# Two product tiles of a sliding-window attention added by an accumulating DMA before TensorE sums them

## The chip, the cores and the metric

The kernel runs on one NeuronCore of a Trainium2 chip. A core has TensorE (PE, matrix products; its weight loads are listed as PEld), VectorE (DVE), ScalarE (ACT), GpSimd (POOL) and SyncE (SP), which run side by side and wait for one another by semaphores. The tensor memory that the engines work in (SBUF, 128 partitions) is filled and emptied by 16 DMA engines; matrix products land in eight banks of PSUM. The metric is the device time of one execution in microseconds; lower is better.

## The reference

One input `x` of 2048 tokens by 1024 features feeds two branches, mixed by a gate:

```python
g = sigmoid((x * gate_w).sum(-1, keepdims=True))
out = g * attention(x, wqkv, wo) + (1 - g) * ffn(B_x, w_gate, w_up, w_down)
# attention: 32 heads of 32; token s looks at s, s-2, ..., s-14 (8 places), where they exist
logits = einsum("bhsd,bhswd->bhsw", q, kg) * Dh ** -0.5     # kg: k gathered at those places
o = einsum("bhsw,bhswd->bhsd", softmax(masked logits), vg)  # then o @ wo
# ffn: (gelu(x @ w_gate) * (x @ w_up)) @ w_down, 3584 hidden features
```

All matrices are bf16. In the kernel both branches work on the same x.

## The kernel before

**Units.** The products of x with the weights are made in 78 units. Each unit makes two tiles of 128 features for 1024 tokens (a half, `s` = 0 or 1) by a scheme with seven products of 4 matmuls each instead of eight. Units 0 and 1 belong to the feed-forward branch; units 2 to 9 make q and k of the first 1024 tokens (one head tile `t` = 0 to 7 in each), units 10 to 17 those of the second half, units 18 to 25 make v, and the rest are feed-forward units. In unit b the order on TensorE is: first product (`p1`, L376, followed by ScalarE's copy L384), two products of the unit before (`p73`, L398, followed by VectorE's L403 that adds and evicts them), one product (`p5`), then a *slot* for one waiting job of another kind (L1260), small jobs for the gate (`gate_chunk` in units 8 and 10), two products (`p26`), and the last product of the unit before (`p4`, L406). q and k are kept in SBUF and stored by GpSimd's queue for a remainder (L529, L530).

**Logits.** For each head tile, VectorE multiplies q with the eight shifted copies of k: three blocks of 256 tokens per half (`ND` = 3), each a tile of 128 x 2048 (`qk_mult`, L598). The sum over the features of a head is made by TensorE against a pattern of ones (`reduce_mm`, L603): 4 matmuls for each block, which write 32 of the 128 output rows each and run beside one another, and which go on adding in the same PSUM bank over the eight head tiles. After two head tiles one slot job is queued; it sums the two tiles of the three blocks, 24 matmuls. A generator `qk_prods` waits until all pairs before it were summed. Six product tiles (`prod_tile`) go round. When all eight tiles of a half are summed, the softmax of that half begins. The fourth block of each half is done later (`spill`).

**Order of the work.** Every engine runs its instructions in the order in which the program emits them, and the program is written out by hand with a small planner: at the end of each unit `run_bg` gives background jobs (generators that emit VectorE work and report its estimated cost) a budget of 4.7 or 4.8 us, and 1.6 us more in a unit with a slot up to unit 21, 0.8 later, 0.6 for a gate job. Jobs go by priority (lowest number first), each from a unit on (`wake`), and some have a due unit at which what is left of them is emitted at once. The overdraft of a unit is taken from the next.

**Weight forms.** `t_forms` (lowest priority, 6) makes from the down and output weights in 9 steps the sums that a later product needs (L874), and GpSimd's queue stores them in DRAM (L877). `tf_load` fetches the weights for a step by SP's queue (L860), into one of three regions of 8 KB per partition that go round (`R_TF`, at 92, 100 and 108 KB) for the first five steps. At the end of unit 13 `tf_close` emits what is left of those five, and the v weights are loaded into the first two regions. VectorE later writes v's own sums from 108 KB on (`sums_v`, units 16 and 17).

**The end of the loop.** After unit 77 `run_last` and `down` multiply the feed-forward and attention results with the down and output weights; before that, VectorE folds the v products (L745, L752), multiplies the last feed-forward results (L254, L257) and scales blocks by the gate (L918).

Of the kernel before, what the change touches and what calls it, by code (L numbers as in the profile page):

```python
# [9 lines left out]
ALU = mybir.AluOpType  # L10
# [8 lines left out]
NWIN = 8  # L19
DIL = 2  # L20
HALO = 16
AC = 256
# [27 lines left out]
R_TF = (92, 100, 108)  # L50
R_TB = (16, 24)
# [2 lines left out]
R_VB = (40, 48.25)  # L54
R_AB = (44.25, 52.5)
R_PROD2 = 56.5
R_BUF = tuple(1 + 18 * k for k in range(10))
R_U2 = 181
R_QS = 189
# [9 lines left out]
def kernel(  # L69
# [12 lines left out]
    nc = tc.nc  # L82
# [7 lines left out]
    NT = KT  # L90
# [16 lines left out]
    def reg3(kb, a, b):  # L107
        return reg(kb, a * b).rearrange("p (a b) -> p a b", a=a)
# [9 lines left out]
    def bank(i):  # L118
        return banks[:, i, :]
# [17 lines left out]
    with tc.manual_schedule(engines={mybir.EngineType.PE, mybir.EngineType.DVE, mybir.EngineType.Activation,  # L137
# [55 lines left out]
        def flat(a):  # L193
            return a.rearrange("p a b -> p (a b)")
# [221 lines left out]
        now = [0]  # L416
# [17 lines left out]
        def bg(gen, prio, wake):  # L434
            t = Task(gen, prio, wake)
            tasks.append(t)
            tasks.sort(key=lambda t_: t_.prio)
            return t
# [41 lines left out]
        def at(n, fn):  # L480
            hooks.setdefault(n, []).append(fn)
# [10 lines left out]
        Q0 = 2  # L492
# [82 lines left out]
        kb = [reg3(R_Q + 9 * i + 4, NT, KV) for i in range(2)]  # L575
        vb = [reg3(R_VB[i], NT, KV) for i in range(2)]
        pr_off = [R_PR + 4 * i for i in range(4)] + [R_PROD + 4 * i for i in range(2)]
        prod = [reg3(o, NWIN, AC) for o in pr_off]
        attn_all = reg3(R_ATTN, NBLK, SC)
        mask = reg3(R_MASK, NWIN, SJ)  # L580
# [11 lines left out]
        def prod_tile():  # L592
            k = pr_n[0] % 6
            pr_n[0] += 1
            return prod[k]
# [5 lines left out]
        def reduce_mm(lg, src, start, stop):  # L601
            for j in range(NJ):
                nc.tensor.matmul(lg[32 * j:32 * j + 32, :], lhsT=R_[:], rhs=src[:, :, j * SJ:(j + 1) * SJ],  # L603
                                 start=start, stop=stop)

        ND = BPS - 1
        LGB = 5
        reduced, front, prods = [0], set(), {}

        def qk_prods(u, s, t):  # L610
            while reduced[0] < NT * s + t - t % 2:
                yield None
            out_ = []
            for a in range(ND):
                pr = prod_tile()
                qk_mult(pr, u.T[:, 0, a * AC:(a + 1) * AC], u.T[:, 1, a * AC:(a + 1) * AC])
                out_.append(pr)
                yield 1.14
            prods[t] = out_
            if t % 2:  # L620
                slotq.append(lambda: (qk_reduce(s, t - 1, prods[t - 1]), qk_reduce(s, t, out_)))

        def qk_reduce(s, t, out_):
            assert s == 0 or t > 0 or front == {0, 2}
            for a, pr in enumerate(out_):
                reduce_mm(bank(LGB + a), pr, t == 0, t == NT - 1)
            reduced[0] += 1
            if t == NT - 1:
                if s == 0:
                    bg(softmax(0, 2, LGB, 0), 1, now[0])  # L630
                    bg(softmax(2, 1, LGB + 2, 1), 1, now[0])
                else:
                    bg(softmax(BPS, 3, LGB, 2), 1, now[0])
# [3 lines left out]
            nc.sync.dma_start(out=kb[s], in_=k_d[s][:])  # L637

        def spill(s):
            while reduced[0] < 2 * NT:  # L640
                yield None
            accs = []
            temps = [prod_tile() for _ in range(2)]

            def mult(t, dst):
                qk_mult(dst, qb[s][:, t, :], kb[s][:, t, HALO:HALO + AC])

            def add(g, t):
                TT(out=accs[g], in0=accs[g], in1=temps[t % 2], op=ALU.add)

            for g in range(NT // QG):
                accs.append(prod_tile())
                mult(QG * g, accs[g])
                yield 1.14
                for t in range(1, QG):
                    mult(QG * g + t, temps[t % 2])
                    yield 1.14
                    if t > 1:
                        add(g, t - 1)
                        yield 1.14  # L660
                add(g, QG - 1)
                yield 1.2
            slotq.append(lambda: spill_reduce(s, accs))

        slotq = []
# [139 lines left out]
        QE = Q0 + 2 * NT  # L805
# [41 lines left out]
        NQ = NK // NP  # L847
        N1 = 5
# [1 line left out]
        TC = NQKV + 1  # L850

        def tf_set(q):
            o = R_TF[q % 3] if q < N1 or q >= N1 + 2 else R_TB[q - N1]
            return [reg3(o + NP * k, NP, SC) for k in range(4)]

        def tf_load(q):
            i0 = NP * q
            for k, a in enumerate(((0, 0), (0, 1), (1, 0), (1, 1))):
                for sl, src in r_parts(*a, i0, i0 + NP):
                    nc.sync.dma_start(out=tf_set(q)[k][:, sl.start - i0:sl.stop - i0, :], in_=src)  # L860
# [3 lines left out]
        def t_forms():  # L864
            for q in range(NQ):
                tf_q[0] = q
                if q in (N1 + 1, N1 + 2):
                    tft.prio = 3.9 if q == N1 + 1 else 4.5
                    tasks.sort(key=lambda t_: t_.prio)
                while q >= N1 and now[0] < (TB if q < N1 + 2 else TC) + 1:  # L870
                    yield None
                r11, r12, r21, r22 = tf_set(q)
                for o_, a, b_ in ((r11, r12, r11), (r12, r22, r12), (r22, r22, r11), (r21, r21, r22)):
                    TT(out=flat(o_), in0=flat(a), in1=flat(b_), op=ALU.subtract)  # L874
                    yield 0.71
                for k, t in enumerate((r11, r22, r12, r21)):
                    nc.gpsimd.dma_start(out=t_d[k][:, NP * q:NP * q + NP, :], in_=t)  # L877
                if q + 3 < (N1 if q < N1 else NQ if q >= N1 + 2 else 0):
                    tf_load(q + 3)

        at(Q0 + 1, lambda: [tf_load(q) for q in range(3)])
        at(TB, lambda: [tf_load(q) for q in range(N1, N1 + 2)])
        at(TC, lambda: [tf_load(q) for q in range(N1 + 2, min(N1 + 5, NQ))])
        tft = bg(t_forms(), 6, Q0 + 2)
# [65 lines left out]

        KX = int(R_P5A[0] - R_BUF[6])

# [296 lines left out]
        for b in range(n):  # L1249
            now[0] = b  # L1250
            for fn in hooks.pop(b, []):
                fn()
            cur = units[b]
            prv = units[b - 1] if b > 0 else None
            cur.p1()
            if prv:
                prv.p73()
            cur.p5()
            extra = 0.0
            if slotq:  # L1260
                slotq.pop(0)()
                extra += 1.6 if b <= QE + 3 else 0.8
            for fn in pre.pop(b, []):
                fn()
                extra += 0.6
            cur.p26()
            while actq and cur.kind != "up":
                actq.pop(0)()
            if prv:
                prv.p4()  # L1270
            for fn in post.pop(b, []):
                fn()
            run_bg(b, (4.7 if b < NQKV else 4.8) + extra)
            if b == n - 1:
                pre_down_4(0)
# [32 lines left out]
```

## Time and profile before

| | |
|---|---|
| median of 3 runs | 720.22 us (719.84 to 720.38) |
| profiled execution | 720.06 us, span 718.3 us |
| TensorE / VectorE / ScalarE / GpSimd busy | 707.2 / 673.2 / 328.7 / 134.5 us |
| granted TensorE clock | 1.00 |
| sum matmuls (L603) | 208, 13.1 us |
| product tiles of the logits (L598) | 64 of 1219 ns |
| SP's queue (q1) / GpSimd's queue (q0) | 105.46 MB / 48.29 MB |

The span is what the profile covers from the first to the last instruction; the execution's own time is 1.8 us longer. In a group's row the numbers after the bar are the busy time of the group (us), the mean of one instruction (ns), and the idle time of the engine before them with what ended it. In the timeline a row is: start (us), length (us), engine, line, operation, output and inputs, count, and in brackets the idle time before it and who ended it. A row of a stretch has its bounds, its length, the busy time of TensorE, its weight loads, VectorE, ScalarE and GpSimd with their counts, the granted clock, the share of the DMA engines' time and the GB/s. In the list of waits a row has the total, the number of times and the longest.

### The profile page before, as it was taken

The numbers are of one execution on the slowest core, as the hardware profiler recorded it, in microseconds if no ns is written. First come the engines' busy times: TensorE is split into PE (matmuls) and PEld (weight loads), VectorE is DVE, ScalarE is ACT, GpSimd is POOL, SyncE is SP. The second block draws the span as 40 slices with busy tenths as digits, with TensorE's granted clock in tenths as the row PEclk, the third lists the DMA queues.
The fourth block names the chain that finished last, engine by engine and source line by source line (L and its number), as shares of the span: only waits on it lengthen the run. The fifth ranks groups of instructions, "written<-read, shape, count | busy, mean of one in ns | idle before, by whom it ended". The sixth has DMA issues, their size and how long they took to land. (4 is left out here: it accounts for less than half of the span.)

```text
span 718.3 us, 10752 instructions
## 1 busy us (share of the span) xinstructions
PE 707.2 (98%) x4051; PEld 408.2 (57%) x4107; DVE 673.2 (94%) x722; ACT 328.7 (46%) x600; POOL 134.5 (19%) x233
## 2 busy tenths in 40 slices
PE   8999999999999999999999999999999999999998
PEld 4466656655544444444444444444447886758887
DVE  2789989999999999999999999999999999899997
ACT  4554546444456665555555555555322321131431
POOL 1323544133210332121300000000210002110011
PEclk9999999999999999999999999999999999999999
DMA  9976643378264758574934836371891899995951
GB/s 276 284 183 219 229 142 122 106 247 304 102 205 127 231 197 252 175 221 149 294 115 152 280 123 214 124 288 59 300 427 52 307 401 396 420 429 223 379 213 60
DMA packets 92276, 162.04 MB, mean 226 GB/s; under 512 B 19280, under 2 KB 68848, under 8 KB 87872
## 3 DMA queue, kind: packets, MB, share of 16 engines
q1 hardware_dynamic: 75520, 105.46, 42.7%
q0 software_dynamic: 15984, 48.29, 19.3%
q10 hardware_dynamic: 720, 7.60, 2.7%
q8 instruction: 32, 0.52, 0.3%
q14 instruction: 20, 0.16, 0.1%
HBM read 112.17 MB, written 54.14 MB: 232 GB/s over the span
## 5 line engine op out<-in xcount | busy, mean ns | idle before, releaser
L366 PE MATMUL banks<-arena 128*128 128x512 bf16 x2136 | 472.1, 379 | 4.2 <-DVE arena L403 0.7
L366 PEld LDWEIGHTS <-arena 128*128 128x128 bf16 x2184 | 240.5, 111 | 235.3 <-issue 7.0
L1046 PE MATMUL banks<-arena 128*128 128x256 bf16 x1260 | 138.9, 273 | 0.8 <-DVE arena L1012 0.6
L1046 PEld LDWEIGHTS <-arena 128*128 128x128 bf16 x1260 | 123.1, 98 | 16.7 <-issue 1.5
L389 ACT COPY arena<-banks 128x512 f32<-128x512 f32 x78 | 45.8, 587 | 130.7 <-PE banks L366 130.7
L403 DVE TENSOR_TENSOR arena<-banks,arena 128x1024 bf16<-128x1024 f32 x78 | 95.2, 1221 | 11.0 <-PE banks L366 5.5
L374 ACT CAST arena<-banks 128x512 bf16<-128x512 f32 x102 | 59.7, 586 | 42.4 <-PE banks L366 42.4
L745 DVE TENSOR_TENSOR arena<-arena 128x2048 bf16<-128x2048 bf16 x64 | 77.0, 1220 | 0.5
L752 DVE TENSOR_TENSOR arena<-arena 128x2048 bf16<-128x2048 bf16 (+2 forms) x96 | 73.9, 776 | 1.0
L598 DVE TENSOR_TENSOR arena<-arena 128x2048 bf16<-128x2048 bf16 x64 | 74.7, 1219 | 0.1
L260 POOL DMA_DIRECT2D h_d<-arena x28 | 20.4, 730 | 226.5 <-DVE arena L254 195.4
L1079 PE MATMUL banks<-arena 128*128 128x512 bf16 x282 | 62.5, 379 | 0.3
L396 ACT COPY banks<-banks 128x512 f32<-128x512 f32 x78 | 44.5, 570 | 21.8 <-PE banks L366 20.0
L1004 DVE TENSOR_TENSOR arena<-arena 128x2304 bf16<-128x2304 bf16 x40 | 53.3, 1352 | 0.5
L384 ACT COPY banks<-banks 128x512 f32<-128x512 f32 x78 | 45.0, 576 | 13.6 <-PE banks L366 12.1
L1051 ACT COPY banks<-banks 128x256 f32<-128x256 f32 x60 | 21.4, 356 | 60.9 <-PE banks L1046 60.7
L1079 PEld LDWEIGHTS <-arena 128*128 128x128 bf16 x288 | 28.2, 98 | 33.5
L927 DVE TENSOR_TENSOR arena<-arena 128x2048 bf16<-128x2048 bf16 (+1 forms) x40 | 41.8, 1111 | 1.3 <-DMA arena<-h_d 1.3
L372 ACT ACTIVATE arena<-banks 128x512 bf16<-128x512 f32 x54 | 32.2, 597 | 15.4 <-PE banks L366 15.3
L323 DVE TENSOR_TENSOR arena<-arena 128x1024 bf16<-128x1024 bf16 x60 | 38.6, 685 | 0.5
L1012 DVE TENSOR_TENSOR arena<-arena 128x2304 bf16<-128x2304 bf16 x28 | 37.7, 1351 | 0.2
L254 DVE TENSOR_TENSOR arena<-arena 128x2048 bf16<-128x2048 bf16 x28 | 34.0, 1216 | 1.9 <-ACT arena L251 1.4
(93 smaller groups left out, 435.8 us busy)
## 6 DMA issues: line engine op xcount, KB each, us to landing
arena<-t_d SPq DMA_DIRECT2D x8, 2304.0 KB, 14.4
h_d<-arena POOLq DMA_DIRECT2D x28, 512.0 KB, 4.3
arena<-w_c SPq DMA_DIRECT2D x12, 1152.0 KB, 14.1
t_d<-arena POOLq DMA_DIRECT2D x36, 256.0 KB, 4.3
arena<-h_d SPq DMA_DIRECT2D x6, 1536.0 KB, 12.7
arena<-in_B_w_gate_dram SPq DMA_DIRECT2D x15, 512.0 KB, 5.7
arena<-in_B_w_up_dram SPq DMA_DIRECT2D x15, 512.0 KB, 5.3
arena<-in_B_w_down_dram SPq DMA_DIRECT2D x28, 256.0 KB, 6.6
```

The source lines that it names most:

```text
L366: self.pe = nc.tensor.matmul(ps, lhsT=self.L[form](kt), rhs=rhs[:, kt, :], start=(start and kt == 0), stop=(kt == HK - 1), skip_group_chec ...
L374: nc.scalar.copy(out=o_, in_=i_)
L384: nc.scalar.copy(out=self.Y, in_=self.X)
L389: nc.scalar.copy(out=self.p5s, in_=self.V)
L396: nc.scalar.copy(out=self.Z, in_=self.Y)
L403: TT(out=self.T[:, :, c2s], in0=pair, in1=self.p5s.rearrange("p (o n) -> p o n", o=1).to_broadcast([P, 2, SC]), op=ALU.add)
L598: TT(out=dst, in0=q.rearrange("p (o s) -> p o s", o=1).to_broadcast([P, NWIN, AC]), in1=_win_ap(k, [[-DIL, NWIN], [1, AC]]), op=ALU.mult)
L745: TT(out=prod2[(t // 2) % 2][:, t % 2], in0=ab, in1=_win_ap(v[:, t, HALO:HALO + AC], [[SJ, NJ], [-DIL, NWIN], [1, SJ]]), op=ALU.mult)
L752: TT(out=out_, in0=h(0), in1=h(1), op=ALU.add)
L1004: TT(out=o_, in0=a, in1=b_, op=op)
L1046: nc.tensor.matmul(c(i, h, j), lhsT=l[:, kt, j * P:(j + 1) * P], rhs=r[:, kt, :], start=False, stop=(kt == KH - 1), skip_group_check=True)
L1079: nc.tensor.matmul(ps, lhsT=L[:, i, j * P:(j + 1) * P], rhs=R[:, i, :], start=(start and q == 0), stop=(q == NK - 1), skip_group_check=not ...
```

## The change

For the four pairs of head tiles of the first 1024 tokens, VectorE writes the products of the odd tile into three tiles of their own (`pr_tmp`, at 108 to 120 KB), and after each of them GpSimd's queue issues a DMA that adds this tile (512 KB, bf16) to the product tile of the even head tile. A job of cost 0 that wakes one unit later puts the pair's sum into the slot queue, so that the sum is emitted one unit later than before; it now has 12 matmuls instead of 24. The pairs of the second half are summed by 24 matmuls as before; the odd tile of its first pair is written to `pr_tmp` too. `qk_prods` may now run ahead of the sums by one pair in the first half and at the start of the second. The third region of the weight forms is given up for `pr_tmp`: the first five steps go round in two regions, two steps are loaded ahead and each further one after the step two before it. A slot of the first half grants 0.8 us to the planner instead of 1.6.

```diff
+R_TMP = 108
...
+        pr_tmp = [reg3(R_TMP + 4 * i, NWIN, AC) for i in range(3)]
...
         def qk_prods(u, s, t):
-            while reduced[0] < NT * s + t - t % 2:
+            pair, add = s * NT // 2 + t // 2, paired(s * NT // 2 + t // 2)
+            while len(reduced) < pair - int(pair <= NT // 2 or t % 2 == 0 and pair == NT // 2 + 1):
                 yield None
             out_ = []
             for a in range(ND):
-                pr = prod_tile()
+                pr = pr_tmp[a] if pair <= NT // 2 and t % 2 else prod_tile()
                 qk_mult(pr, u.T[:, 0, a * AC:(a + 1) * AC], u.T[:, 1, a * AC:(a + 1) * AC])
                 out_.append(pr)
+                if add and t % 2:
+                    nc.gpsimd.dma_start(out=flat(prods[t - 1][a]), in_=flat(pr), accum_op=ALU.add)
                 yield 1.14
             prods[t] = out_
             if t % 2:
-                slotq.append(lambda: (qk_reduce(s, t - 1, prods[t - 1]), qk_reduce(s, t, out_)))
...
+                if add:
+                    bg(later(lambda p=prods[t - 1]: qk_reduce(s, pair, [p])), -1, now[0] + 1)
+                else:
+                    slotq.append(lambda p=prods[t - 1]: qk_reduce(s, pair, [p, out_]))
+
+        def paired(pair):
+            return pair < NT // 2
+
+        def later(fn):
+            slotq.append(fn)
+            yield 0.0
+
+        def qk_reduce(s, pair, sets):
+            assert pair == len(reduced)
+            p = pair % (NT // 2)
+            assert s == 0 or p > 0 or front == {0, 2}
+            for k, out_ in enumerate(sets):
+                for a, pr in enumerate(out_):
+                    reduce_mm(bank(LGB + a), pr, p == k == 0, p == NT // 2 - 1 and k == len(sets) - 1)
+            reduced.append(pair)
...
         def tf_set(q):
-            o = R_TF[q % 3] if q < N1 or q >= N1 + 2 else R_TB[q - N1]
+            o = R_TF[q % 2] if q < N1 else R_TF[q % 3] if q >= N1 + 2 else R_TB[q - N1]
...
-                if q + 3 < (N1 if q < N1 else NQ if q >= N1 + 2 else 0):
-                    tf_load(q + 3)
...
+                m_ = 2 if q < N1 else 3
+                if q + m_ < (N1 if q < N1 else NQ if q >= N1 + 2 else 0):
+                    tf_load(q + m_)
...
-        at(Q0 + 1, lambda: [tf_load(q) for q in range(3)])
+        at(Q0 + 1, lambda: [tf_load(q) for q in range(2)])
...
-                extra += 1.6 if b <= QE + 3 else 0.8
+                extra += 1.6 if b <= QE + 3 and len(reduced) > NT // 2 else 0.8
```

More of the change, by code (lines that the diff above doesn't have):

```diff
@@ L607 @@
         LGB = 5
-        reduced, front, prods = [0], set(), {}
+        reduced, front, prods = [], set(), {}
         def qk_prods(u, s, t):
-            while reduced[0] < NT * s + t - t % 2:
+            pair, add = s * NT // 2 + t // 2, paired(s * NT // 2 + t // 2)
+            while len(reduced) < pair - int(pair <= NT // 2 or t % 2 == 0 and pair == NT // 2 + 1):
                 yield None
@@ L620, in qk_prods @@
             if t % 2:
-                slotq.append(lambda: (qk_reduce(s, t - 1, prods[t - 1]), qk_reduce(s, t, out_)))
[L623 to L628, printed above, removed]
+                if add:
[15 more added lines that the diff above has]
+            reduced.append(pair)
+            if p == NT // 2 - 1:
                 if s == 0:
@@ L639, in spill @@
         def spill(s):
-            while reduced[0] < 2 * NT:
+            while len(reduced) < NT:
                 yield None
```

## The prediction

> **What bounds the kernel now.** I read the page's busy times first, then who waited for whom on TensorE, the groups by line, and the timeline and the stretches of the part that is changed (48 to 118 us).
>
> ```profile
> PE 707.2 (98%) x4051; PEld 408.2 (57%) x4107; DVE 673.2 (94%) x722; ACT 328.7 (46%) x600; POOL 134.5 (19%) x233
> ...
> L598 DVE TENSOR_TENSOR arena<-arena 128x2048 bf16<-128x2048 bf16 x64 | 74.7, 1219 | 0.1
> ...
> L603 PE MATMUL banks<-arena,ones_r 128*32 128x512 bf16 x208 | 13.1, 381 | 0.0
> ```
> TensorE works 98% of the span and VectorE 94%: two engines are nearly full, and a gain on one lasts only while the other follows. All 208 sum matmuls cost 13.1 us, four at a time; the 48 that go are part of that.
>
> ```profile
> PE banks L366 <- DVE arena L403: 0.7, 2, 0.5
> ```
> That is the longest wait of the unit loop's matmuls: TensorE bounds it, VectorE is close behind.
>
> ```profile
> 57.36 3.49 DVE L598 TENSOR_TENSOR arena<-arena 128x2048 bf16<-128x2048 bf16 x3
> 57.74 0.56 POOL L529 DMA_DIRECT2D q_d<-arena  x1 [2.22 <-DVE arena L403]
> 58.29 0.56 POOL L530 DMA_DIRECT2D k_d<-arena  x1
> ...
> 60.52 0.57 ACT L384 COPY banks<-banks 128x512 f32<-128x512 f32 x1
> ...
> 62.26 1.23 DVE L403 TENSOR_TENSOR arena<-banks,arena 128x1024 bf16<-128x1024 f32 x1
> 62.95 0.98 PEld L603 LDWEIGHTS <-ones_r 128*32 128x32 bf16 x24 [0.38 <-issue]
> 62.95 1.48 PE L603 MATMUL banks<-arena,ones_r 128*32 128x512 bf16 x24
> ...
> 64.36 0.44 PE L366 MATMUL banks<-arena 128*128 128x512 bf16 x1
> ```
> This is the first pair's slot, in unit 6. The odd tile's three products end at 58.58, 59.72 and 60.85, and TensorE sums at 62.95. A slot of 24 matmuls takes 62.95 to 64.36, 1.41 us. It begins 2.43 us after the L384 copy that follows a unit's first product, and L384 recurs every 6.05 us (54.48, 60.52) without a slot.
>
> ```profile
> 55.00:60.00 5.00, 4.95 (x24) 3.31 (x24) 4.63 (x13) 2.19 (x5) 1.63 (x3) 1.00 1.08 355
> 60.00:65.00 5.00, 5.00 (x41) 2.76 (x40) 4.88 (x6) 1.56 (x5) 1.22 (x3) 1.00 0.08 28
> 76.60:90.70 14.10, 13.84 (x91) 8.73 (x95) 13.18 (x15) 6.82 (x15) 6.27 (x12) 1.00 0.57 185
> 520.00:600.00 80.00, 79.89 (x619) 60.58 (x619) 78.34 (x78) 21.91 (x52) 4.57 (x9) 1.00 0.76 303
> ```
> The last two columns are the DMA engines' share and GB/s. The queues are free right after 60, but over half full at 77 to 91, where later additions run. The last row gives the rate of full engines: 303/0.76 = 399 GB/s.
>
> **The change part by part.** *Removed:* 12 of 24 sum matmuls in four slots. At 1.41 us for 24, half is 0.70: 4 x 0.70 = 2.8 us off TensorE, which waits there for nothing (2.6 if some 0.05 a slot is fixed). VectorE's products stay the same 48 + 16.
>
> *Added: twelve additions of 512 KB on GpSimd's queue.* Issue: 0.54 to 0.86 us each on an engine that is 19% busy, hidden; behind them in GpSimd's order stand the q and k stores and the t stores. No addition by DMA is in the trace. Copying 512 KB takes all DMA engines 1.31 us at 399 GB/s; the h store that ran alone (487 to 491 us) held them 37.8% of 4 us, 1.51 us. An addition must fetch both tiles, so twice that: 2.6 or 3.0. From below, a plain copy: 1.3. From above, the transposing DMA that also handles its data: 13 of 128 KB (512 tokens by 128 features) in 18.48 us of SP's queue, 5.7 us per 512 KB. I take 2.6, since the destination is SBUF as for the loads of that row; 3.0, 1.3 and 5.7 stay for the range. The fixed part is 1.9 us: a q store of 64 KB lands 2.1 us (median) after its issue and moves for 0.2.
>
> The Trainium skill ("Collectives: The Full Stack", The bandwidth ceiling) says that a reduction runs at half the copy's rate because the add needs two source reads, not because adding costs cycles. By that the two-fold price holds; by the bare copy each addition would be 1.3 us and the sum 0.4 us lower. No run here has shown either.
>
> *Moved: each pair's sum goes one unit later* (units 7, 9, 11, 13), and this is the time that the DMA has. With half slots of 0.70 and the gate matmuls of units 8 and 10 at 0.71 (slot and gate together held 76.60 to 78.72), L384 of unit 7 falls at 66.72 (68.13 less 1.41), of units 9, 11, 13 at 80.23, 93.74, 106.54. The third tile's sum begins 2.43 + 0.47 later: 69.6, 83.1, 96.6, 109.4. The odd tile's first product ends at 58.6, and for the others 4.12 after L384 of units 7, 9, 11 (1.74 to L403, 1.14, 1.22): 70.8, 84.3, 97.9. Time allowed: 11.0, 12.3, 12.3, 11.6 us. Needed: 0.3 behind the k store + 1.9 + 3 x 2.6 = 10.0, plus what competes: nothing for the first (share 0.08); for the others the four 256 KB weight loads that the change puts there, 2.6 us at 399 GB/s, of which about 2.3, 2.3 and 2.0 fall beside them. Margins 1.0, 0.0, 0.0, -0.4: TensorE waits 0.4 us. Every 0.1 us on an addition adds 0.3 us to three or four pairs.
>
> *Weight forms with two buffers instead of three.* Sets 2, 3, 4 are loaded one form later, each behind t stores that stand in the software queue after the additions. At unit 9 the first form of set 3 comes at about 88 us, and its second load lands about then. VectorE may be 1.4 us late in a unit (L403 can start 1.74 after L384 and takes 1.22; TensorE needs it 20 matmuls, 4.4 us, after L384) and 2.1 with a gate. I take 0, bounds 0 and 2. The v weights wait for the t stores of set 4 at unit 13 as before (second load at 121.75, first use at 133.72): 6 us of cover.
>
> *Planner.* Four slots grant 0.8 us less background work, so 3.2 us of VectorE pieces slide back to the end of the loop, where VectorE has no room:
>
> ```profile
> 508.89 1.22 DVE L403 TENSOR_TENSOR arena<-banks,arena 128x1024 bf16<-128x1024 f32 x1
> ...
> 510.16 2.75 PE L366 MATMUL banks<-arena 128*128 128x512 bf16 x12 [0.28 <-DVE arena L403]
> ```
> Working the planner's accounts through, unit 76 gets one more v product and two more folds (1.1 + 0.7 + 0.4) ahead of this L403 and loses one scaling (1.1): L403 comes 1.1 us later against TensorE, and the 0.28 wait grows by up to that. I take 0.8, ends 0 and 1.1. Until there VectorE follows: from 145 to 505 us it stands idle before L403 and the softmax for some 6 us, more than 2.8. After the loop VectorE waits for the last h load until 534.10, while TensorE has work that needs none of it until 544.68. In the second half pair 5 sums in unit 16 instead of 17, with its products two units old; 0.
>
> *Sum:* -2.8 + 0.4 + 0.8 = -1.6 us. The profiled execution took 720.06 (span 718.3 and 1.8 around it), 0.16 under the median of 720.22: 718.5 profiled, **718.6** against the median.
>
> **Rivals.** (1) *The additions land late*: this one ends on the other side. Place: the half slots, where TensorE would wait for a DMA. At 3.0 us an addition the waits are 0.2 + 1.2 + 1.2 + 1.6 = 4.2; they also give VectorE its time, so without the 0.8: -2.8 + 4.2 = +1.4, 721.6. At 4.4 they are 21: 738. At 5.7, 36.6: 754. It takes the whole gain from about 2.8 us, and shows as slower from 3.0. For it: margins of nothing in three pairs, and the h store's 1.51. Against it: full-rate rows at 399 GB/s and a quiet queue after 60. (2) *VectorE gives the gain back*: it is at 235.6 of 240 us in the middle of the kernel, and with every earlier TensorE time met by a late L403, the saving shrinks to 0 to 1: 719.4 to 720.2. Against it: its idle before L403 is there to be eaten. (3) *The form loads stall VectorE* at units 9 and 13 by 5 us: beyond the cover of 2.1, 3 us each: -1.6 + 6 = 724.6. For it: the t stores now stand behind the additions. Against it: form work stands last in VectorE's order.
>
> **How the numbers follow.** A change under 0.2% (1.4 us) can't be told from none. In time, with its own range of 717.4 to 720: 0.43. A little late (2.8 to 4.4 us an addition): 0.26. Far late: 0.18. VectorE gives it back: 0.07. Form loads: 0.06. Predicted is the first case, the likeliest single one. About four in five of it end below 718.8: faster 0.35; its rest, rival 2 and a trace of rival 1 are the same: 0.16; slower 0.49. Range 717.4 (a plain copy's price, no loss at the end) to 738, which leaves out the far late additions.
>
> **What would show it.** Half slots of L603, 12 matmuls in 0.70 us, with no TensorE wait on a DMA before them; additions landing within 10 to 12.3 us of the first product's end, three in a row some 2.6 us apart; L403 near the end of the unit loop with a wait of about 1 us. Wrong if the additions land more than 3 us apart (rival 1), if L366 waits for L403 all along (rival 2), or if L874 waits for weight loads (rival 3).

## The result and the profile after

| | before | after |
|---|---|---|
| median | 720.16 us (4 runs, 719.84 to 720.38) | 729.04 us (4 runs, 727.60 to 729.83) |
| profiled execution | 720.06 us, span 718.3 | 729.21 us, span 727.1 |
| TensorE / VectorE / GpSimd busy | 707.2 / 673.2 / 134.5 us | 711.6 / 673.2 / 145.0 us |

The changed kernel takes 1.0121 times as long, with a 95% interval of 1.0104 to 1.0139: 8.9 us slower. A gain of 1.6 us was forecast. VectorE does the same work. TensorE's busy time grows although 48 matmuls are gone. A part of the growth is a stretch at half the clock (below). Another part is no work at all: 48 records of L366 are missing in the profile of before (2136 against 2184), and their time is not counted as busy. From 240 to 480 us, where TensorE's work is unchanged, the profile of before has 1097 matmuls and 238.84 us, that of after 1119 and 240.00. For the same reason the count of instructions does not show the 48.

The busy times of the page and the group of the product tiles, after:

```profile
PE 711.6 (98%) x4059; PEld 408.4 (56%) x4059; DVE 673.2 (93%) x722; ACT 328.9 (45%) x600; POOL 145.0 (20%) x245
...
L600 DVE TENSOR_TENSOR arena<-arena 128x2048 bf16<-128x2048 bf16 x64 | 74.8, 1219 | 0.1
```

The product tiles still take 1219 ns, so neither the added DMAs nor their issue slow these products. What is new stands in the list of TensorE's waits (total, times, longest; L605 are the sum matmuls, L367 the products of a unit, L283 the gate's matmuls, L1065 the matmuls behind the loop):

```profile
PE banks L605 <- DMA arena<-arena: 4.5, 3, 2.1
PE banks L1065 <- DVE arena L1031: 1.8, 2, 1.2
PE banks L367 <- DVE arena L404: 1.8, 2, 1.0
PE banks L283 <- ACT arena L390: 1.3, 2, 0.7
```

The first row is the additions: the sums of three tiles stand still for them. Before, L366's wait for L403 was 0.7 in all, and there was no wait of the gate's matmuls.

The stretches of the changed part, after (bounds, length, busy times of TensorE, weight loads, VectorE, ScalarE, GpSimd, then the granted clock, the DMA engines' share and GB/s):

```profile
76.60:90.70 14.10, 12.68 (x72) 7.51 (x71) 9.66 (x10) 6.75 (x15) 7.14 (x13) 1.00 0.99 269
60.00:80.00 20.00, 19.33 (x103) 12.07 (x102) 19.28 (x21) 9.66 (x22) 10.06 (x16) 1.00 0.95 215
80.00:100.00 20.00, 18.58 (x99) 11.27 (x97) 15.29 (x17) 9.04 (x21) 11.75 (x21) 1.00 1.01 256
100.00:140.00 40.00, 35.47 (x189) 21.16 (x188) 34.05 (x37) 17.70 (x34) 19.01 (x33) 0.96 0.77 232
```

From 60 to 100 us the DMA engines have hardly anything free: 0.95 and 1.01, where the kernel before shows 0.61 and 0.39; from 100 to 140 it is 0.77, before 0.36. The 76.60 row had 0.57 before. The GB/s rise less than the share, since an addition holds the engines for longer than the bytes counted for it.

The first pair's half slot, in the timeline after:

```profile
67.84 0.57 ACT L385 COPY banks<-banks 128x512 f32<-128x512 f32 x1
...
70.27 0.88 PE L605 MATMUL banks<-arena,ones_r 128*32 128x512 bf16 x12
```

It begins 2.43 us after L385, as forecast, and waits for nothing. The third tile of pair 2 (the pairs are counted from 0) waits, and so does the last pair, pair 3, here with the rows behind it:

```profile
102.91 0.40 PE L605 MATMUL banks<-arena,ones_r 128*32 128x512 bf16 x4 [2.07 <-DMA arena<-arena]
...
115.47 0.40 PE L605 MATMUL banks<-arena,ones_r 128*32 128x512 bf16 x4
116.26 0.40 PE L605 MATMUL banks<-arena,ones_r 128*32 128x512 bf16 x4 [0.38 <-DMA arena<-arena]
118.74 0.62 PE L605 MATMUL banks<-arena,ones_r 128*32 128x512 bf16 x4 [2.08 <-DMA arena<-arena]
...
119.29 3.02 PE L367 MATMUL banks<-arena 128*128 128x512 bf16 x8
```

In pair 3 the second and third tile wait 0.38 and 2.08 us. Then eight matmuls take 3.02 us (0.38 each), while elsewhere twelve take 2.75 (0.23 each). The granted clock says why, in the stretch of just this time (the last but two column):

```profile
118.10:121.50 3.40, 2.76 (x10) 1.05 (x10) 3.23 (x7) 0.25 (x1) 2.57 (x6) 0.50 0.97 354
```

It is at half from 118.1 to 121.5 us, for 3.41 us in the records.

**Where the 8.9 us are.** L384 (now L385) recurs once in a unit, so its distance from unit to unit, after less before, gives an account:

| place | us |
|---|---|
| start, up to unit 0 | +1.3 |
| four slots of 24 gone (1.56 each), four of 12 come (0.97 each) | -2.4 |
| gate matmuls in units of their own | +2.0 |
| unit 9: L404 late (wait 0.74) | +0.8 |
| sums wait for additions: 2.07 in unit 11, 0.38 and 2.08 in unit 13 (4.5, 4.8 with what restarts) | +4.8 |
| half clock in units 13 to 15 | +1.4 |
| waits of before that are gone (118.78 and 175.74 us, and a 0.1) | -0.9 |
| end of the loop (0.73) and behind it (1.15), less 0.1 | +1.8 |

A unit without a slot takes 6.05 us, with a slot of 24 it takes 7.61, with one of 12 it takes 7.02. The start is not the change: over the profiled executions of the kernels of this study the copy of unit 0 lies anywhere between 25.9 and 27.5 us, with 26.14 before and 27.41 after. It goes with the time at which the full clock is first granted: 8.9 to 9.3 us in the three executions with 27.4 or 27.5 (the change, runs 1 and 2 below), 4.0 to 7.2 in all others.

Three of these lines need the profile. First the gate in unit 8 and the form loads in unit 9, from the timeline after:

```profile
78.03 0.61 PE L283 MATMUL banks<-arena 128*32 128x512 bf16 x8 [0.67 <-ACT arena L390]
...
85.06 0.69 DVE L892 TENSOR_TENSOR arena<-arena 128x1024 bf16<-128x1024 bf16 x1 [3.84 <-DMA arena<-in_B_w_down_dram]
...
86.95 1.22 DVE L404 TENSOR_TENSOR arena<-banks,arena 128x1024 bf16<-128x1024 f32 x1
88.22 4.48 PE L367 MATMUL banks<-arena 128*128 128x512 bf16 x20 [0.74 <-DVE arena L404]
```

The gate's eight matmuls wait 0.67 us for ScalarE's copy of a bank (L390). Before, the slot's sum matmuls ran ahead of them and covered this wait. VectorE stands 3.84 us for a weight load of `tf_load`, then 0.60 for another; L404 is late, and TensorE waits. These loads were issued from 73.4 us on, beside the second pair's additions, and three of the four took 9.7 to 10.5 us. One issued at 103.58, when the additions had landed, took 3.0.

Second, GpSimd's own waits between 60 and 125 us, from the list of waits and the timeline after:

```profile
POOL z_d L288 <- DMA arena<-arena: 6.5, 3, 3.2
...
POOL t_d L895 <- DMA arena<-arena: 1.9, 1, 1.9
...
POOL k_d L531 <- DMA arena<-arena: 0.8, 1, 0.8
```

```profile
100.68 0.48 POOL L288 DMA_DIRECT2D z_d<-arena  x1 [3.23 <-DMA arena<-arena]
...
103.14 0.48 POOL L288 DMA_DIRECT2D z_d<-arena  x1 [1.98 <-DMA arena<-arena]
...
107.56 2.70 POOL L622 DMA_DIRECT2D arena<-arena  x3
```

The z stores read a small tile that no addition touches. The additions of pair 2 landed at 96.66, 100.40 and 102.86, and the z stores that leave 0.3 us after each stand eight places behind it in the queue. The trace's records show why. The DMAs of GpSimd's queue tell of their landing by eight semaphores that go round (numbers 111 to 118), and each DMA first waits for the one that had its semaphore before: the store at 96.94 waits for semaphore 115, which the addition issued at 89.85 raises. So it is the program that lets no ninth transfer of this queue start while the oldest of eight is under way. Before, the same eight go round. The queue stood 9.2 us behind additions in all; 6.5 of them, at the z stores, lie ahead of the last pair's additions, which left at 107.56, though the first odd product was ready at 101.78. Before, GpSimd's only wait for a transfer here is 0.6 us, of a load for the store whose data it reads.

Third, the end of the loop and the work behind it, after:

```profile
518.01 2.75 PE L367 MATMUL banks<-arena 128*128 128x512 bf16 x12 [1.01 <-DVE arena L404]
...
589.38 2.79 PE L1065 MATMUL banks<-arena 128*128 128x256 bf16 x24 [1.15 <-DVE arena L1031]
```

The first was 0.28 before; the second is new.

### The profile page after: what moved, and what is told of

Same layout as the page of the kernel before. It is cut to its first block, busy times and chain, and to the rows that moved or that the text cites. A ratio compares the mean times of both kernels' runs of the same rounds, so it can differ in the third digit from the quotient of the medians.

```text
span 727.1 us, 10734 instructions
## 1 busy us (share of the span) xinstructions
PE 711.6 (98%) x4059; PEld 408.4 (56%) x4059; DVE 673.2 (93%) x722; ACT 328.9 (45%) x600; POOL 145.0 (20%) x245
## 5 line engine op out<-in xcount | busy, mean ns | idle before, releaser
L367 PE MATMUL banks<-arena 128*128 128x512 bf16 x2184 | 476.2, 380 | 2.2 <-DVE arena L404 1.8
L367 PEld LDWEIGHTS <-arena 128*128 128x128 bf16 x2184 | 240.5, 111 | 236.9 <-issue 9.2
L1065 PE MATMUL banks<-arena 128*128 128x256 bf16 x1260 | 138.9, 273 | 1.8 <-DVE arena L1031 1.8
L1065 PEld LDWEIGHTS <-arena 128*128 128x128 bf16 x1260 | 123.0, 98 | 17.8 <-DVE arena L1031 1.4
L404 DVE TENSOR_TENSOR arena<-banks,arena 128x1024 bf16<-128x1024 f32 x78 | 95.2, 1221 | 15.1 <-PE banks L367 11.6
L390 ACT COPY arena<-banks 128x512 f32<-128x512 f32 x78 | 45.8, 587 | 130.8 <-PE banks L367 130.8
L600 DVE TENSOR_TENSOR arena<-arena 128x2048 bf16<-128x2048 bf16 x64 | 74.8, 1219 | 0.1
L385 ACT COPY banks<-banks 128x512 f32<-128x512 f32 x78 | 45.0, 576 | 13.6 <-PE banks L367 12.4
L1031 DVE TENSOR_TENSOR arena<-arena 128x2304 bf16<-128x2304 bf16 x28 | 37.8, 1355 | 0.2
```

Of the source, the lines that this page charges most:

```text
L367: self.pe = nc.tensor.matmul(ps, lhsT=self.L[form](kt), rhs=rhs[:, kt, :], start=(start and kt == 0), stop=(kt == HK - 1), skip_group_chec ...
L385: nc.scalar.copy(out=self.Y, in_=self.X)
L390: nc.scalar.copy(out=self.p5s, in_=self.V)
L404: TT(out=self.T[:, :, c2s], in0=pair, in1=self.p5s.rearrange("p (o n) -> p o n", o=1).to_broadcast([P, 2, SC]), op=ALU.add)
L600: TT(out=dst, in0=q.rearrange("p (o s) -> p o s", o=1).to_broadcast([P, NWIN, AC]), in1=_win_ap(k, [[-DIL, NWIN], [1, AC]]), op=ALU.mult)
L1065: nc.tensor.matmul(c(i, h, j), lhsT=l[:, kt, j * P:(j + 1) * P], rhs=r[:, kt, :], start=False, stop=(kt == KH - 1), skip_group_check=True)
```

## The experiments

Theories, by the names that the expectations use. *Crowding* or *engine* theory: additions and their neighbours share DMA engines that are full. *Issue* or *queue* theory: GpSimd's queue, behind the additions, sends stores and later additions too late. *Rhythm* theory: the loss comes from moving and halving the sums (gate matmuls, weight forms, half slots), with no part of the DMA. *Planner* theory: the end of the loop loses because a half slot grants 0.8 us instead of 1.6. The kernel before was timed with each group: 720.04, 720.06, 719.93 and 719.94 us. Waits, clocks and rows are those of the one profiled execution of a run; its time is given where it lies 1 us or more from the median.

**1. A plain copy instead of the addition.** The even tiles' products are lost; the DMA has one tile to read instead of two.

```diff
-  nc.gpsimd.dma_start(out=flat(prods[t - 1][a]), in_=flat(pr), accum_op=ALU.add)
+  nc.gpsimd.dma_start(out=flat(prods[t - 1][a]), in_=flat(pr))
```

> The changed kernel with the adding taken out of the twelve DMAs: each copies the odd tile over the even one (the even tiles' products are lost from the logits). Same issues, same bytes written, half the bytes read. Crowding theory (the additions hold the DMA engines 2.56 us each; weight loads and GpSimd's queue stand behind them): the copies land about 1.4 us apart, no TensorE wait on a DMA, the form wait of 4.4 us shrinks under 2, and of the 8.9 us over the kernel before 5 to 7 go: about 722 to 724. Rhythm theory (moved sums, gate matmuls without cover, planner order): hardly a change, 727 to 729. Issue theory (the twelve issues on GpSimd are the cost, whatever they move): 727 to 729 as well, with the same gaps in GpSimd's queue.

Measured: 721.64 us (10 runs; profiled 725.03, with a wait of 2.01 us at 367.74, far behind the changed part), 1.0028 [1.0016, 1.0041]. The copies of pair 0 land 1.48 and 1.47 us apart, those of pair 3 1.29 and 1.21, about half of what the additions of these pairs show. TensorE waits for none of the copies, the clock stays at 1.00, and the stretches from 60 to 100 us show how far the engines are from full:

```profile
60.00:80.00 20.00, 19.22 (x102) 11.99 (x103) 19.33 (x20) 9.61 (x22) 8.04 (x16) 1.00 0.78 281
80.00:100.00 20.00, 19.22 (x109) 11.54 (x109) 16.15 (x18) 9.67 (x22) 12.74 (x25) 1.00 0.80 276
```

Same queue, same moved sums, and twelve issues as before, though each takes GpSimd 0.54 us here and 0.89 with the addition: some 7 us of the 8.9 hang on what an addition costs beyond a copy, and that is above all the time that it holds the DMA engines.

**2. No DMA at all.** The odd tiles are computed and left out of the sums.

```diff
-  if add and t % 2:
-      nc.gpsimd.dma_start(out=flat(prods[t - 1][a]), in_=flat(pr), accum_op=ALU.add)
```

> The changed kernel without the twelve DMAs; the sums take the even tiles alone (the odd tiles' products of the first 1024 tokens are left out of the logits). What the halved and moved sums, the two form regions and the planner give by themselves. Crowding theory: -2.4 for the half slots, +1.5 for gate matmuls that now wait for a copy in units 8 and 10, +1 to 2 at the end of the loop: 720.5 to 722. Prediction's sum without any DMA: -2.8 + 0.8 = 718.2. Rhythm theory: over 726.

Measured: 722.31 us (720.36 to 725.10, 10 runs), 1.0030 [1.0016, 1.0043]. With the additions free the kernel is still not faster than before. Its TensorE waits are the gate's 0.67 twice, 1.00 at L404 near the end of the loop and 1.02 at L1063 behind it. The saved 2.4 us are spent on these.

**3. The delay alone.** No DMA, as in 2; TensorE sums both tiles with 24 matmuls, one unit later.

```diff
-  bg(later(lambda p=prods[t - 1]: qk_reduce(s, pair, [p])), -1, now[0] + 1)
+  bg(later(lambda p=prods[t - 1]: qk_reduce(s, pair, [p, out_])), -1, now[0] + 1)
```

> No DMA, but all 24 matmuls in the four slots, one unit later than before; output as the reference's. The price of the delay, the regions and the planner alone, without the saving. Crowding theory: 2.4 more than the run without DMA and half the sums, so 723 to 724.5. If the moved order costs nothing by itself: 720 to 721.

Measured: 723.67 us (6 runs), 1.0046 [1.0030, 1.0062]. In unit 18 the profiled execution stands 1.99 us behind before (2.04 less 0.05 of start): the price of the two gate units, 1.0 each, and nothing else up to there. Near and behind the end of the loop 1.00 and 0.75 follow.

**4. Three form regions.** The product tiles of the odd heads get room of their own, and the weight forms keep their third region; all else as changed.

```diff
-R_TMP = 108
+R_TMP = (73, 77, 116, 108)
...
-            o = R_TF[q % 2] if q < N1 else R_TF[q % 3] if q >= N1 + 2 else R_TB[q - N1]
+            o = R_TF[q % 3] if q < N1 or q >= N1 + 2 else R_TB[q - N1]
```

> The changed kernel with the third region of the weight forms given back (the tiles for the odd products lie at 73, 77 and 116 KB instead). Additions as they are. Crowding theory: VectorE's wait of 4.4 us for form weights at unit 8 goes, the third pair's additions start 3 to 4 us earlier, its wait of 2.07 goes or falls under 0.5, and the late L403 of 0.74 goes: 725 to 727. If the buffers had no part in it: 728 to 729.

Measured: 727.23 us (4 runs; profiled 726.22), 1.0099 [1.0076, 1.0121]. VectorE's waits for forms are gone. The median is 1.8 us below that of the change, but the two intervals overlap, so the size is not sure. TensorE's waits for additions, of which one was to go, stay at 4.6 us (2.15, 0.17, 2.32), and so does a half clock of 3.41 us.

**5. Stores off GpSimd's queue.** The t stores of the first five forms and the z stores of chunks 2 and 3 go to SP's queue.

```diff
-  nc.gpsimd.dma_start(out=t_d[k][:, NP * q:NP * q + NP, :], in_=t)
+  (nc.sync if q < N1 else nc.gpsimd).dma_start(out=t_d[k][:, NP * q:NP * q + NP, :], in_=t)
...
```

> The changed kernel with the t stores of the first five form steps and the gate stores of units 8 and 10 issued from SP's queue instead of GpSimd's; two form regions, additions on GpSimd. Queue theory (GpSimd has at most eight DMAs on the way, so behind three additions its queue stands until they land, and the next pair's additions are issued late): GpSimd's waits for additions (9 us in the changed kernel) go, the additions of pairs 3 and 4 start within 1.5 us of their products, TensorE waits under 1.5 us for DMAs instead of 4.5, and the slow clock after them goes: 721.5 to 724.5. Engine theory (the DMA engines themselves are full, whoever issues): the additions land as late as before, 726 to 729.

Measured: 732.44 us (6 runs; profiled 736.34), 1.0165 [1.0150, 1.0180], 3.4 us slower than the change. TensorE's waits here, and GpSimd's row ahead of the last pair's additions:

```profile
PE banks L605 <- DMA arena<-arena: 6.8, 4, 2.8
PE banks L1065 <- DVE arena L1031: 3.9, 2, 3.3
```

```profile
108.32 0.76 POOL L299 DMA_DIRECT2D zc<-z_d  x1 [7.42 <-DMA z_d<-arena]
```

Four sums wait instead of three. But the move did not free GpSimd's queue: the copy `zc` on it waits 7.42 us for z stores that leave SP's queue only at 104.62 us and later, and the additions behind it left at 109.07, 8.4 us after their first product (100.67). So for the last pair this run does not test the queue theory. Pair 2 does: its additions left 0.6 us after the first product (88.10 and 87.55), the last landed 15.0 us after it, and the sum waited 2.76. There the queue was not late, and the DMA engines, as full as ever (1.01 and 1.02 from 60 to 100 us), were enough. The queue theory falls as the whole cause.

**6. Gate jobs in the units of the half slots** (7 and 9 instead of 8 and 10).

```diff
-  at_slot(Q0 + 6, lambda: gate_chunk(2, bank(1)))
+  at_slot(Q0 + 5, lambda: gate_chunk(2, bank(1)))
...
```

> The changed kernel with the two gate jobs moved from units 8 and 10, which have no slot now, to units 7 and 9, behind the half slots. Both theories: the two waits of TensorE for the copy L390 before the gate matmuls (0.67 each) go, and the gate stores no longer stand behind the additions of the third pair; so 1.3 us by the gates alone (727.5), and by the queue theory 2 to 4 us more because the fourth pair's additions are issued earlier (724 to 726).

Measured: 730.18 us (4 runs), 1.0131 [1.0114, 1.0149]. The gate waits are gone as said, and nothing is won: the earlier TensorE waits longer for additions (0.89, 2.09, 1.07, 2.28), and VectorE's waits for forms grow to 8.4 us, one of which reaches TensorE with 2.48.

**7 and 8. All three mends**, at first with the planner's 0.8 for a half slot, then with the full credit:

```diff
-  extra += 1.6 if b <= QE + 3 and len(reduced) > NT // 2 else 0.8
+  extra += 1.6 if b <= QE + 3 else 0.8
```

> Three form regions, t and gate stores on SP's queue, gates in the half slots, additions as in the change. If the chain of causes is complete (form wait, queue, gates, slow clock), what is left is -2.4 for the half slots and +1.5 to 2 for VectorE at the end of the loop: 719.3 to 720.5. If the DMA engines are too full, TensorE still waits 1 to 3 us for additions: 721.5 to 724.

> The same, and the planner grants 1.6 us in the half slots as before, so no VectorE work slides to the end of the loop. Planner theory: the wait before L404 near 516 us and the one before L1031 near 587 shrink to 0.3 and 0, and 1.5 us go against the run without this: 718 to 719. If VectorE is the true bound, those waits only move to units 8 to 16: no gain against it.

Measured: 726.75 us (6 runs; profiled 724.77), 1.0087 [1.0064, 1.0109], and 726.70 us (6 runs; profiled 725.40), 1.0090 [1.0067, 1.0114]. In 7 the first addition of the last pair leaves 1.3 us after its product (100.91 and 99.61), those of the other pairs within 0.6: the queue is no longer late, and the sums still wait 3.1 us. L404 waits 1.01 at the end of the loop and L1065 3.5 behind it. In 8 these last two are 0.28 and nothing: the planner theory holds for them. But the sums wait 0.73, 1.15 and 2.98 there, and a half clock of 3.41 us follows, which the profiled execution of 7 is without. The medians are the same. That a saving ahead of a full DMA path is waited away at the next addition fits this, but rests on one profiled execution of each: in each version four of the six runs have a mean clock of 0.995 to 0.999.

**9. No additions, with the three regions, the gate jobs in the half slots and the full credit.** The odd tiles are left out of the sums, as in 2.

> No additions (the odd tiles' products are written but left out of the sums), three regions for the weight forms, the gate jobs in the units of the half slots, and the planner's full 1.6 for a half slot. Rhythm and planner theories together: what the run without DMA lost against its saved matmuls is the two waits of the gate jobs (0.67 each) and the two waits at the end of the loop (1.0 each, 0.3 before); with these gone, four slots save 0.59 each: 720.1 - 2.4 = 717.7, between 717.2 and 718.8, faster than before. Rival: the loss lies in something else that goes with fewer sum matmuls (VectorE as the bound): 720 to 722 again.

Measured: 718.04 us (8 runs), 0.9977 [0.9967, 0.9987]: 1.9 us faster than before. TensorE's waits in the profile are those of the kernel before (L367 for L404: 0.9 in three, longest 0.5; none at the gate). The gate units, the regions and the credit together explain what run 2 lost; they are not told apart here. About 2.4 us saved, four half slots of 0.59, is what the idea can give at most, when additions cost nothing.

**10. Sums two units later** than the products instead of one, nothing else.

```diff
-  bg(later(lambda p=prods[t - 1]: qk_reduce(s, pair, [p])), -1, now[0] + 1)
+  bg(later(lambda p=prods[t - 1]: qk_reduce(s, pair, [p])), -1, now[0] + 2)
```

> The changed kernel with each pair's sum two units later instead of one (units 8, 10, 12, 14), nothing else. Engine theory: the additions have 6 us more, so TensorE's three waits for them (4.5 us) and the half clock behind them (1.7) go; the gate jobs of units 8 and 10 get a slot ahead of them again (1.3). The form wait of unit 8 (0.7) and the waits at the end of the loop (2.2) stay: 729.0 - 7.5 = 721.5, between 720.5 and 723. Queue theory: what GpSimd's queue holds up (the stores of z, and the last additions, then beside the v weights) comes later too, and a wait takes their place: 725 or more.

Measured: 736.01 us (4 runs; profiled 737.50), 1.0222 [1.0208, 1.0236]. The 721.5 of the engine theory failed by 14 us, though its first half was right: no sum waits for an addition. The queue theory's 725 or more came, by a wait that it had not named. From the timeline:

```profile
122.97 0.69 DVE L892 TENSOR_TENSOR arena<-arena 128x1024 bf16<-128x1024 bf16 x1 [12.32 <-DMA arena<-in_B_w_down_dram]
...
124.85 2.72 PE L367 MATMUL banks<-arena 128*128 128x512 bf16 x6 [10.82 <-DVE arena L404]
```

The weight load of the fifth form goes into a region that is free only when the t stores of two forms before have landed. These stand behind additions on GpSimd's queue; the loads left at 115.08. VectorE stands 12.3 us, TensorE 10.8, and the granted clock is 0.83 from 100 to 140 us.

**11. Two units later, three regions, full credit.**

> Sums two units later, three regions for the weight forms and the planner's full 1.6. Engine, issue and planner theories together: no wait for additions, for forms or at the end of the loop is left beyond those of the kernel before: 721.5 - 0.7 - 1.5 = 719.3, between 718 and 720.5; faster than or the same as before. If GpSimd's queue (stores behind additions) or the shared DMA engines bring waits in other places or a half clock: 723 or more.

Measured: 724.72 us (7 runs; profiled 728.39, the slowest of the seven), 1.0060 [1.0047, 1.0074]: the expectation's second case, waits in other places. No sum and no form waits for a transfer, and still it is 4.8 us slower. Now it is the gate's copy `zc`, which GpSimd's queue sends behind the z stores, and these behind additions:

```profile
107.41 0.22 DVE L301 TENSOR_REDUCE zs<-zc 128x8 f32<-128x32 f32 x1 [2.82 <-DMA zc<-z_d]
...
114.27 2.10 PE L367 MATMUL banks<-arena 128*128 128x512 bf16 x9 [2.80 <-DVE arena L404]
```

VectorE also waits 1.2 us for an addition to leave a product tile and 1.7 for a v weight load, and L1065 2.57 us for L1031 behind the loop, in spite of the full credit, with a half clock of 3.41 us behind it; why that one is there was not settled.

**12. Only the first pair added by DMA**, the others summed by 24 matmuls; three regions, full credit.

```diff
-            return pair < NT // 2
+            return pair == 0
```

> Only the first pair's tiles are added by DMA (three additions, at 60 to 71 us, where the queues were quiet before); the other pairs are summed by 24 matmuls in their old units. Three regions for the weight forms and the planner's full 1.6. Engine theory: 10 us for an allowed 11, no wait, the gate jobs keep their slots: -0.6 for the half slot, 719.5, between 718.8 and 720.3, not to be told from before. Rival (any three additions crowd out weight loads or stores): 721 or more.

Measured: 721.29 us (11 runs), 1.0016 [1.0007, 1.0024]. No sum waits for an addition; one waits 0.42 us for VectorE's products, at 92.35. TensorE loses 1.18 us to L404 once, at 115.95, behind this wait of VectorE:

```profile
DVE zs L301 <- DMA zc<-z_d: 1.0, 1, 1.0
```

The 16 KB copy `zc` was issued at 102.27 us, just behind a 1 MB weight load from 102.26, and took 5.5 us; before it left 0.8 us ahead of that load and took 2.3. Three additions at 60 to 70 us leave the later order of issues a little changed, and by this one execution that is enough to eat a gain of 0.6. The expected 719.5 did not come; the rival's 721 did.

**13. GpSimd adds the tiles itself**, with the three mends; this takes the additions off the DMA engines.

```diff
-  nc.gpsimd.dma_start(out=flat(prods[t - 1][a]), in_=flat(pr), accum_op=ALU.add)
+  nc.gpsimd.tensor_tensor(out=flat(prods[t - 1][a]), in0=flat(prods[t - 1][a]), in1=flat(pr), op=ALU.add)
```

> The twelve additions are made by GpSimd itself (a sum of two 128 x 2048 bf16 tiles) instead of a DMA, with the three mends (three regions for the weight forms, gate jobs in the units of the half slots, full 1.6). Engine theory: the DMA engines are what was too full, so with the additions elsewhere the 717.9 of the run without additions comes back if one addition on GpSimd takes under some 3.5 us: 718 to 719, faster than or the same as before. Rival: GpSimd takes over 4 us for one, or holds up VectorE, which is 94% busy, while it adds: TensorE waits for the last addition of each pair or for L404, 722 or more. VectorE's product tiles (1.22 us alone) will show the second.

Measured: 770.74 us (5 runs), 1.0703 [1.0688, 1.0718]: the rival was right, by far more than it said. The groups by form between 55 and 140 us on VectorE, one row of the timeline, and the group on GpSimd:

```profile
L892 DVE TENSOR_TENSOR arena<-arena 128x1024 bf16<-128x1024 bf16 x16 | 42.6, 2678 | 0.2
L600 DVE TENSOR_TENSOR arena<-arena 128x2048 bf16<-128x2048 bf16 x22 | 33.4, 1568 | 0.0
```

```profile
113.25 12.90 DVE L892 TENSOR_TENSOR arena<-arena 128x1024 bf16<-128x1024 bf16 x1
```

```profile
L622 POOL TENSOR_TENSOR arena<-arena 128x2048 bf16<-128x2048 bf16 x12 | 52.7, 4422 | 0.3 <-DVE arena L600 0.3
```

One addition takes GpSimd 4.4 us. Beside it a form's sum on VectorE, 0.69 us elsewhere, takes 2.7 on average and 12.9 once. L404 is late, TensorE waits 44.7 us for it in seven places, 32.8 of them in three up to 140 us, and its clock falls to 0.74 from 60 to 80 us. The Trainium skill ("SBUF — State Buffer", Who interferes with whom) says that VectorE and GpSimd share one pair of ports and hold it exclusively; the trace agrees in so far as one VectorE instruction is held for as long as three of GpSimd's take (12.90 us against some 12); the ports themselves no trace shows.

No version that keeps all the sums beats the kernel before. The nearest is the first pair alone, 1.4 us slower in the median. Whether more than eight semaphores for GpSimd's queue would help was not tried.

## Why the prediction was wrong

**The half slots: mechanism right, size off.** They saved 0.59 us each, not 0.70. The fixed part of a slot that the forecast held at 0.05 is about 0.4: of 1.56 us for 24 matmuls, 0.97 stay for 12. In all 2.4 instead of 2.8.

**The price of an addition: right for one that has the engines to itself.** On quiet queues they land 2.59 us apart (65.09, 67.68), later 2.56 and 2.47 (113.66, 116.22, 118.69): the 2.6 worked out as two copies of 1.31. But the prediction set "more than 3 us apart" as the sign that it is wrong, and that sign came: 3.03 behind the q and k stores in pair 0, 3.45 and 3.28 in pair 1, 3.74 in pair 2. Over all eight distances the mean is 2.95. The Trainium skill's factor of two for the added source read ("Collectives: The Full Stack", The bandwidth ceiling) is borne out by this and by the copies of run 1 (1.21 to 1.48 us apart on quiet queues); that it is the read which costs, no run shows by itself.

**The margins: this step failed.** From the first odd product's end to the last landing:

| pair | forecast needed | forecast allowed | measured needed |
|---|---|---|---|
| 0 | 10.0 | 11.0 | 10.9 (59.86 to 70.71) |
| 1 | 12.3 | 12.3 | 12.9 (71.94 to 84.84) |
| 2 | 12.3 | 12.3 | 13.6 (89.31 to 102.86) |
| 3 | 12.0 | 11.6 | 16.9 (101.78 to 118.69) |

The forecast put the sum of these waits at 0.4 us; they were 4.5. Pair 0 made it by about 0.1 us instead of 1.0; pair 1 by about 0.5, only because the gate in unit 8 had made its sum later. Two things were left out. The competition was counted as the bytes of four weight loads only, while q, k, t and z stores shared the engines too: the first addition of pair 2 took 6.8 us to land where one alone took 4.7. And the issue on GpSimd, "hidden" at 19% busy, was not: the queue stood 6.5 us at the z stores, each waiting for one of the program's eight semaphores, so pair 3 began 5.8 us late. That the busy share of GpSimd was low said nothing about how long its queue stands. The late queue is not needed for waits, though: in run 7 additions leave within 1.3 us of their products, and the sums still wait 3.1 us.

**Rival 1 came.** Its mechanism (TensorE waits in the half slots) is what happened. It was to decide from 2.8 to 3.0 us an addition: alone an addition takes 2.6, with its neighbours it came to 2.95 in the mean. At 3.0 it forecast waits of 4.2 us, and 4.5 were measured, but in other pairs: none in the first two, and in the last one with the late queue. Its total of +1.4 us was too small, since the gate matmuls and the half clock were not in it. The half clock, 1.4 us, was in no case of the forecast. The Trainium skill ("TensorE: Matmul & The Clock Gate", What's actually happening) has the clock at half after an idle window of about 3.4 us; the trace agrees in the length, 3.41 us, but here no single wait was longer than 2.1.

**Two form regions: costed at 0, bound 2, measured 0.8.** It hit by the loads of set 2, at 85 us, where the first form of set 3, at 88, was expected to be critical; VectorE stood 4.4 us, beyond the cover of 2.1. By run 4 it is some 1.8 us with what follows, with overlapping intervals. This is rival 3's mechanism, once and for 0.8 us instead of twice for 3.

**The gate matmuls: an unnamed term.** They were taken at 0.71 without a slot. The time of slot and gate together (76.60 to 78.72) was known, but that the slot covered the wait for L390 was not seen: a gate alone costs 1.0 more than one in a slot, 2.0 for two. Run 3 has this term by itself, run 9 is without it.

**Planner: first half right.** L404's wait near the end of the loop grew by 0.73, forecast 0.8. That VectorE's backlog costs nothing behind the loop was wrong: 1.15 us at 589.38. Run 8 takes both away.

Sum by the measured terms without DMA: -2.4 + 2.0 + 1.8 = +1.4, before any addition is late. The forecast's -1.6 could not have come even with additions for nothing: run 2's span, 720.7, is 2.4 over that of before, 1.4 of it at the start.

## What to carry to other kernels

Before work is moved to DMA, count the transfers of every queue in that stretch, with the time that they hold the engines, and ask what the issuing queue does when its oldest transfer is slow, and how many semaphores the program gives it; an issuing engine that is 20% busy can still be late by 6 us. When an instruction block is taken away or halved, look at what waited behind its cover: here two small gate jobs lost almost all that the halved sums saved. A change that saves 0.3% at best needs every one of these to be zero.

## What the runs showed of the hardware that was not expected

- An accumulating DMA of 512 KB within the tensor memory in a row with others lands every 2.47 to 2.59 us on quiet queues, where a copy of its size needs 1.21 to 1.48 (run 1). Its issue takes GpSimd 0.89 us instead of 0.54. Beside additions three weight loads of 256 KB took 9.7 to 10.5 us, one behind them 3.0.
- What looks like a full queue can be the program's own: stores of 2 KB left 0.3 us after an addition eight places ahead, because eight semaphores go round in GpSimd's queue and each DMA waits for the one before it on its semaphore. What the queue itself would take was not tested.
- Waits of 0.38 and 2.08 us, with short sum matmuls between, brought a half clock of 3.41 us, which began within the second. One wait of 2.57 us (run 11, 586.14) was followed by one too, while single waits of 2.07 us (102.91) and 2.80 us (run 11, 114.27) brought none. The half clocks within the spans of the change and of runs 4, 5, 6, 8, 10 and 11 last 3.41, 6.83 or 13.65 us. What decides between a half clock and none was not settled.
- A sum on GpSimd holds up VectorE's sums of two bf16 tiles: those of the forms take 2.7 us instead of 0.69 on average, and 12.9 at most; the product tiles 1.57 instead of 1.22.
